# Four small moves in a fused retention and feed-forward kernel: attention of chunks 2 to 5 a tile later, one batch's transposes behind a matmul tile, one weight load triggered sooner, a last store of 128 columns

## The chip, the cores and the metric

The kernel runs on one core of a Trainium2 chip. The metric is the time of one execution on the device in microseconds (us). Six runs of the kernel before gave a median of 211.3 us, from 210.18 to 211.53. One further look at one execution, taken by the hardware profiler, gives the trace that this text reads.

## What is computed

Retention (a linear attention with a decaying state) over 4 batches, 8 heads, 768 positions and 64 dimensions a head; its output, with the heads side by side, is the 3072 x 512 input of a feed-forward layer with a tanh-approximated GELU:

```python
state = gamma * state + einsum('bhd,bhe->bhde', k[t], v[t])      # per head, for every t
y[t]  = scale * einsum('bhd,bhde->bhe', q[t], state)
x = y.transpose(0, 2, 1, 3).reshape(3072, 512)
h = x @ w_in                                                    # 512 -> 2048
out = gelu_tanh(h) @ w_out                                      # 2048 -> 512
```

## The kernel before, in words

**Tiling.** The 768 positions are cut into 6 chunks (c = 0 to 5) of 128; every chunk holds 4 batches (b), so 512 tokens. Per chunk the kernel does the attention in chunked form and then the two feed-forward products, M1 (x @ w_in, then GELU) and M2 (g @ w_out). The attention of chunk c + 1 is woven into the matmuls of chunk c, so that TensorE always has feed-forward tiles to work on while VectorE (DVE), ScalarE (ACT) and GpSimd (POOL) do the small steps of attention.

**Attention of one batch of one chunk.** `mm_T` transposes q and k on TensorE (chunks 0 and 1; from chunk 2 on `load_blk` loads q and k in blocks, POOL scales them in `prep_blk`, and `tr` transposes on DVE, L261). `mm_A` (L268) multiplies k and q into the scores, `ev_A` (L282) masks them on DVE, `mm_yc` (L289) adds what the state gives, `mm_yi` (L304) what the scores give, `ev_Y` (L317) copies the result into `xT`, which M1 reads; `mm_S` (L322) and `ev_S` (L340) make the next state, `decay` (L354) scales it on POOL. `att_AY` (L380) puts the scores of some batches and the outputs of others together, `att_Y` (L368) the outputs and states of all four.

**M1 and M2.** `moe1` (L452) and `moe1_two` (L457) make one M1 tile: matmuls into a PSUM bank and one GELU on ACT. `moe1_two` covers two column blocks for two batches: 8 matmuls of 256 columns. `units2` (L622) cuts the M2 work of one batch into 4 units of 4 matmuls of 512 columns; after the last of the four, `ev_O` (L495) copies the result to SBUF and stores it. `moe2_last` (L509) does the last batch of chunk 5 in two halves of 256 columns, each copied by DVE and stored by SP.

**What sets the order.** The program runs under a manual schedule: each engine does its instructions in the order in which the text emits them. `run(units, after)` (L521) emits a list of units, and behind unit i whatever the dictionary `after` has under i. In chunks 2 to 4 the units 0 to 15 are M1 tiles and 16 to 31 are M2 units. Loads of q, k and v sit on SP's queue (`load1`, `load_blk`, `load`), some on ACT's; the weights and most stores sit on POOL's, so that triggering a weight load is an instruction among POOL's other work. `hold` (L122, used at L609) makes SP's loads of chunk 1 wait until the third part of w_out has landed.

**The places that the change touches.**

- L545 to L551, on POOL: the first part of w_in is triggered, then k of batches 2 and 3 of chunk 0 is scaled (`prep1`, L195), then the other weight parts are triggered. Parts 0 and 1 of w_in are the two halves of the contraction rows of M1's first four column blocks: `m1a` (L594) uses part 0, and behind the attention of batch 3 part 1.
- L638 to L652: M2 of chunk 0 with attention of chunk 1. Behind its last unit come `att_AY` (which makes the y of batch 1, copied by ACT), `att_T(1, 3)` and `ev_S(1, 1)`.
- L671 to L687: M1 of chunk 1, first for batches 0 and 1, then for batches 2 and 3, 8 tiles each.
- L688 to L699 and L703 to L720: M2 of chunk 1, and chunks 2 to 4.
- L509 to L519: the last batch of the last chunk.

Of the kernel before, what the change touches and what calls it, by code (L numbers as in the profile page):

```python
# [16 lines left out]
def kernel(  # L17
# [14 lines left out]
    n_tok, d_model = out.shape  # L32
# [25 lines left out]
    att = ctx.enter_context(tc.tile_pool(name="att", bufs=4))  # L58
# [30 lines left out]
    def ld_tile(nm, c, b):  # L89
        if nm == "q":  # L90
            t = ld_all(("q32", c)).rearrange("p (b hp) a d -> p b (hp a d)", b=B)
            return t[:, b].rearrange("p (h d) -> p h d", h=H)
        if (nm, c, b) not in raw:
            raw[nm, c, b] = ld.tile([128, H, Dh], F32, tag=f"{nm}32", bufs=6, name=f"{nm}32")
        return raw[nm, c, b]
# [87 lines left out]
    def prep1(eng, nm, c, b):  # L183
        t = pre.tile(
            [128, H, Dh], F16, tag=f"{nm}16", bufs=6 if nm == "q" else 2 * B, name=f"{nm}16"
        )
        src = ld_tile(nm, c, b)
        if nm == "v":
            if eng is nc.scalar:
                eng.copy(out=t, in_=src)  # L190
            else:
                eng.tensor_copy(out=t, in_=src)  # L192
        else:
            col = OQ if nm == "q" else OK
            eng.tensor_tensor(  # L195
                out=t,
                in0=src,
                in1=cst[:, col:col + H].unsqueeze(2).broadcast_to([128, H, Dh]),
                op=ALU.mult,
            )  # L200
        h16[nm, c, b] = t
# [30 lines left out]
    def bank(tag, dt=F32, shape=(128, NHP, 128), name="ps"):  # L232
        return psum.tile(list(shape), dt, tag=tag, bufs=BANKS[tag], name=name)
# [168 lines left out]
    w_in_part = [(i, k, k + 2) for i in range(2) for k in (0, 2)]  # L402
# [14 lines left out]
    def load_w_in(n):  # L417
        i, k0, k1 = w_in_part[n]
        nc.gpsimd.dma_start(
            out=w_in_sb[n],  # L420
            in_=moe_w_in.rearrange("(kc p) (i n) -> p kc i n", p=128, i=NI)[:, k0:k1, i],
        )
# [29 lines left out]
    def moe1(c, fc):  # L452
        h_ps = bank("h", shape=(128, B * C), name="h_ps")
        moe1_mm(c, fc, h_ps, 0, B * C)
        gelu(g_tile(c, fc)[:, fc % 2], h_ps)
# [22 lines left out]
    def moe2_mm(ps, c, b, fcs, n0, n1):  # L478
        for fc in fcs:
            nc.tensor.matmul(  # L480
                out=ps[:, n0:n1],
                lhsT=g_sb[c, fc // 2][:, fc % 2, b * C:(b + 1) * C],
                rhs=w_out_sb[fc // (NF // NO)][:, fc % (NF // NO), n0:n1],
                start=(fc == 0),
                stop=(fc == NF - 1),
            )
# [21 lines left out]

    def moe2_last(c, b):  # L509

        hw = d_model // 2
        rows = out[b * S + c * C:b * S + (c + 1) * C, :]
        o_sb = op.tile([128, d_model], F32, tag="o", name="o_sb")
        for i in range(2):
            ps = bank("h", shape=(128, d_model), name="o_ps")
            m0, m2 = i * hw, (i + 1) * hw
            moe2_mm(ps, c, b, range(NF), m0, m2)
            nc.vector.tensor_copy(out=o_sb[:, m0:m2], in_=ps[:, m0:m2])  # L518
            nc.sync.dma_start(out=rows[:, m0:m2], in_=o_sb[:, m0:m2])  # L519

    def run(units, after):  # L521
        for i, u in enumerate(units):
            u()
            for f, *args in after.get(i, ()):
                f(*args)

    VE, AC, PO, SY = nc.vector, nc.scalar, nc.gpsimd, nc.sync
# [16 lines left out]
    nc.gpsimd.tensor_copy(out=misc[0:1, 4:5], in_=ld_tile("k", 0, 2)[0:1, 0, 0:1])  # L544
    load_w_in(0)  # L545
    prep1(PO, "k", 0, 2)
    prep1(PO, "k", 0, 3)
    for i in range(1, len(w_in_part)):
        load_w_in(i)
    for i in range(NO):  # L550
        load_w_out(i)  # L551
# [70 lines left out]
    def units2(c, b, n=4, tag="o"):  # L622
        u = [(lambda i=i: moe2(c, b, range(i, i + n), tag)) for i in range(0, NF, n)]
        last = u[-1]
        u[-1] = lambda: (last(), ev_O(c, b))
        return u
# [6 lines left out]
    for nm, b in (  # L633
# [12 lines left out]
            14: [(prep1, AC, "v", 1, 2), (att_T, 1, 2), (preps, 1, 3), (ev_S, 1, 0)],  # L646
            15: [
                (att_AY, 1, (1,), "h", 1, (2,), AC),
                (att_T, 1, 3),
                (ev_S, 1, 1),  # L650
            ],
        },  # L652
# [12 lines left out]
    def prep(c, nms):  # L665

        for nm in nms:
# [7 lines left out]
            for fp in range(NF // 2)  # L675
        ],
        {
            0: [(prep1, AC, "v", 1, 3)],
            1: [(att_AY, 1, (2,), "o", 1, (3,), VE)],
            3: [(ev_S, 1, 2)],  # L680
            4: [(att_AY, 1, (3,), "o", 1, (), VE)],
            6: [(ev_S, 1, 3)],
            7: [(prep, 2, "Q")],
            8: [(tr, 2, "q")],
# [4 lines left out]
        [x for b in range(B) for x in units2(1, b)],  # L689
        {  # L690
            1: [(tr, 2, "k", 0, 1)],
            3: [(att_AY, 2, (), "att", 2, (0, 1), None), (tr, 2, "k", 2, 3)],
            7: [(att_AY, 2, (), "att", 2, (2, 3), None)],
            12: [(att_Y, 2), (ev_S, 2, 0)],
            13: [(ev_S, 2, 1)],
            14: [(ev_S, 2, 2)],
            15: [(ev_S, 2, 3)],
        },
    )  # L699

# [1 line left out]
    for c in range(2, NCk - 1):  # L702
        n = c + 1  # L703
        after = {
            2: [(prep, n, "QKvk"), (tr, n, "q")],
            9: [(load, n + 1)] if n + 1 < NCk else [],
            16: [(tr, n, "k", 0, 1)],
            19: [(att_AY, n, (), "att", n, (0, 1), None), (tr, n, "k", 2, 3)],
            23: [(att_AY, n, (), "att", n, (2, 3), None)],
            27: [(att_Y, n)],  # L710
            28: [(ev_S, n, 0)],
            29: [(ev_S, n, 1)],
            30: [(ev_S, n, 2)],
            31: [(ev_S, n, 3)],
        }
        run(
            [(lambda fc=fc: moe1(c, fc)) for fc in range(NF)]
            + [x for b in range(B) for x in units2(c, b)],
            after,
        )  # L720
# [3 lines left out]
    for b in range(B - 1):  # L724
        for x in units2(c, b):
            x()
    moe2_last(c, B - 1)


# [28 lines left out]
```

## Time and profile before

| what | value |
|---|---|
| median of 6 runs (lowest to highest) | 211.3 us (210.18 to 211.53) |
| the profiled execution | 211.53 us, of which its span is 209.5 us |
| TensorE (PE) busy | 202.8 us, 97% of the span |
| DVE / ACT / POOL busy | 91.3 / 83.6 / 101.2 us |
| granted TensorE clock | 1.0 |
| matmuls of M1 (L435) and M2 (L480) | 84.7 and 86.8 us busy |
| DMA | 33.85 MB, mean 162 GB/s; 52.4% of the 16 engines' span on SP's queue |

A row of the timeline has the start in us from the span's start, the duration in us, the engine, the line, the operation with output and inputs, the shape and the count; in brackets stands how long the engine was idle before it, and what ended that. "PE" are matmuls, "PEld" weight loads, "SPq" the triggers of SP's DMA queue. Matmuls are pipelined: a row's duration reaches past the start of the next.

### The profile page before, as it was taken

How to read it: one execution, taken by the hardware profiler on the slowest of the kernel's cores; microseconds unless marked ns; L12 is line 12 of the kernel's file. 1: busy time of each engine (PE TensorE's matmuls, PEld its weight loads, DVE VectorE, ACT ScalarE, POOL GpSimd, SP SyncE). 2: the span in 40 equal slices, each digit the busy share in tenths (PEclk: the TensorE clock that was granted, in tenths of full speed). 3: DMA queues.
4: the chain of work that ended last, by engine and by line, in shares of the span. 5: the costliest groups of instructions: out<-in, count | busy, mean ns of one | idle time of the engine just before them, and what ended most of it. 6: DMA issues, size and time to landing. Idle time of an engine off the chain costs nothing.

```text
span 209.5 us, 4015 instructions
## 1 busy us (share of the span) xinstructions
PE 202.8 (97%) x1582; PEld 109.0 (52%) x1582; DVE 91.3 (44%) x163; ACT 83.6 (40%) x142; POOL 101.2 (48%) x123
## 2 busy tenths in 40 slices
PE   7996999999999999999999999999999999999994
PEld 2455544466888446444446444446444446444453
DVE  6698100188752774531776442476641472100001
ACT  2283662144656113466113466113466113466120
POOL 3597600325373966862958956681558821100100
PEclk9999999999999999999999999999999999999999
DMA  6999999997968999788989889989889121100112
GB/s 157 287 243 168 206 206 201 279 238 129 173 98 184 255 215 212 161 134 154 249 161 212 170 128 214 235 156 212 169 178 237 32 105 50 50 0 3 50 50 100
DMA packets 132691, 33.85 MB, mean 162 GB/s; under 512 B 126528, under 2 KB 130880, under 8 KB 132672
## 3 DMA queue, kind: packets, MB, share of 16 engines
q1 hardware_dynamic: 115248, 21.27, 52.4%
q0 software_dynamic: 5696, 8.91, 18.5%
q10 hardware_dynamic: 11728, 3.41, 7.1%
q8 instruction: 12, 0.20, 0.4%
q14 instruction: 7, 0.06, 0.1%
HBM read 31.48 MB, written 6.29 MB: 180 GB/s over the span
## 4 chain that ended last, share of the span: by engine, by line
PE 86%; DMA 10%; DVE 1%; POOL 1%; ACT 0%; issue 0%; SPq 0%
PE h_ps L435 39%; PE o_ps L480 39%; DMA k<-in_k_dram 5%; DMA w_in<-in_moe_w_in_dram 3%; PE a_ps L273 2%; PE y_ps L308 2%; DMA v<-in_v_dram 2%; PE y_ps L295 2%; PE s_ps L330 1%; POOL k L195 1%; PE qkT_ps L239 1%; DVE st L349 0%; DVE qkT L226 0%; ACT v L190 0%; DVE q L195 0%
## 5 line engine op out<-in xcount | busy, mean ns | idle before, releaser
L480 PE MATMUL o_ps<-w_out,g 128*128 128x512 f16 (+1 forms) x400 | 86.8, 371 | 0.0
L435 PE MATMUL h_ps<-xT,w_in 128*128 128x512 f16 (+1 forms) x464 | 84.7, 342 | 1.7 <-DMA w_in<-in_moe_w_in_dram 1.7
L450 ACT ACTIVATE g<-h_ps 128x512 f16<-128x512 f32 x96 | 56.8, 597 | 47.6 <-PE h_ps L435 47.5
L435 PEld LDWEIGHTS <-w_in 128*128 128x128 f16 x464 | 45.0, 98 | 39.5 <-DMA w_in<-in_moe_w_in_dram 1.8
L480 PEld LDWEIGHTS <-g 128*128 128x128 f16 x400 | 37.9, 98 | 41.0
L286 DVE TENSOR_TENSOR a_sb<-a_ps,mask 128x512 f16<-128x512 f32 x48 | 30.1, 683 | 15.0 <-PE a_ps L273 14.9
L502 ACT COPY o_sb<-o_ps 128x512 f32<-128x512 f32 x19 | 11.1, 586 | 58.1 <-PE o_ps L480 58.1
L195 POOL TENSOR_TENSOR k<-k,cst 128x512 f16<-128x512 f32 x23 | 23.8, 1056 | 12.3 <-DMA k<-in_k_dram 12.3
L507 POOL DMA_DIRECT2D out_dram<-o_sb x18 | 10.0, 559 | 34.6 <-ACT o_sb L502 23.9
L206 POOL TENSOR_TENSOR kT<-kT,cst 128x512 f16<-128x512 f32 x16 | 16.3, 1048 | 13.7 <-DMA kT<-in_k_dram 8.2
L356 POOL TENSOR_TENSOR stg<-st,cst 128x512 f32<-128x512 f16 x16 | 16.3, 1037 | 9.7 <-DVE st L349 8.0
L263 DVE STREAM_TRANSPOSE qkT<-kT 128x512 f16<-128x512 f16 x16 | 10.9, 697 | 16.2 <-POOL kT L206 16.2
L206 POOL TENSOR_TENSOR q<-q,cst 128x512 f16<-128x512 f32 x16 | 16.2, 1044 | 2.5 <-DMA kT<-in_k_dram 2.5
L263 DVE STREAM_TRANSPOSE qkT<-q 128x512 f16<-128x512 f16 x16 | 11.4, 711 | 14.0 <-POOL q L206 14.0
L349 DVE TENSOR_TENSOR st<-s_ps,stg 64x256 f16<-64x256 f32 x32 | 13.4, 420 | 0.8
L192 POOL CAST v<-v 128x512 f16<-128x512 f32 x16 | 9.6, 614 | 8.3 <-DMA v<-in_v_dram 8.2
L195 DVE TENSOR_TENSOR q<-q,cst 128x512 f16<-128x512 f32 x8 | 6.2, 769 | 17.0 <-DMA q<-in_q_dram 17.0
L226 DVE CAST xT<-y_ps 128x512 f16<-128x512 f32 x11 | 7.2, 687 | 14.0 <-PE y_ps L308 14.0
L518 DVE COPY o_sb<-o_ps 128x256 f32<-128x256 f32 x2 | 0.8, 425 | 26.6 <-PE o_ps L480 26.6
L171 PE MATMUL spin_ps<-zero 128*128 128x512 f16 x30 | 10.4, 493 | 1.3 <-DVE zero L139 1.3
L224 ACT CAST xT<-y_ps 128x512 f16<-128x512 f32 x13 | 7.2, 588 | 5.2 <-PE y_ps L308 5.1
L273 PE MATMUL a_ps<-qkT 64*128 64x128 f16 x192 | 8.1, 218 | 0.2
(39 smaller groups left out, 83.3 us busy)
## 6 DMA issues: line engine op xcount, KB each, us to landing
v<-in_v_dram SPq DMA_DIRECT2D x21, 256.0 KB, 4.5
k<-in_k_dram SPq DMA_DIRECT2D x20, 256.0 KB, 4.3
out_dram<-o_sb POOLq DMA_DIRECT2D x18, 256.0 KB, 3.1
q<-in_q_dram SPq DMA_DIRECT2D x64, 64.0 KB, 3.0
kT<-in_k_dram SPq DMA_DIRECT2D x64, 64.0 KB, 2.6
w_out<-in_moe_w_out_dram POOLq DMA_DIRECT2D x4, 512.0 KB, 15.8
q<-in_q_dram ACTq DMA_DIRECT2D x4, 256.0 KB, 7.8
k<-in_k_dram ACTq DMA_DIRECT2D x4, 256.0 KB, 7.6
```

Source lines behind the costliest of these rows:

```text
L171: nc.tensor.matmul(out=ps, lhsT=zero[:, 0:128], rhs=zero, start=True, stop=True)
L195: eng.tensor_tensor(out=t, in0=src, in1=cst[:, col:col + H].unsqueeze(2).broadcast_to([128, H, Dh]), op=ALU.mult,)
L206: nc.gpsimd.tensor_tensor(out=t, in0=ld_all((key, c))[:, b * NHP:(b + 1) * NHP].rearrange("p hp a d -> p (hp a) d"), in1=cst[:, col:col + ...
L263: nc.vector.transpose(out=qkT_tile(c, b)[:, "qk".index(nm)].rearrange("p hp t -> p (hp t)"), in_=blk16.pop((nm, c, b)).rearrange("p ha d - ...
L273: nc.tensor.matmul(out=ps[j][:, hp], lhsT=t[j * 64:(j + 1) * 64, 1, hp], rhs=t[j * 64:(j + 1) * 64, 0, hp], start=True, stop=True,)
L286: nc.vector.tensor_tensor(out=s, in0=ps[j], in1=mask[:, j], op=ALU.mult)
L349: nc.vector.tensor_tensor(out=st[sl, :, b, sl], in0=s_ps[sl], in1=stg[sl, :, b, sl], op=ALU.add)
L356: nc.gpsimd.tensor_tensor(out=stg[:, :, b], in0=st[:, :, b], in1=cst[:, OG:OG + NHP].unsqueeze(2).broadcast_to([128, NHP, 128]), op=ALU.mult,)
L435: nc.tensor.matmul(out=out, lhsT=w_in_of(fc, kc), rhs=xT[c][:, kc, t0:t1], start=(kc == 0 and first), stop=(kc == NHP - 1), skip_group_che ...
L450: nc.scalar.activation(out=out, in_=in_, func=AF.Gelu_apprx_tanh, scale=1.0)
L480: nc.tensor.matmul(out=ps[:, n0:n1], lhsT=g_sb[c, fc // 2][:, fc % 2, b * C:(b + 1) * C], rhs=w_out_sb[fc // (NF // NO)][:, fc % (NF // NO ...
L502: nc.scalar.copy(out=o_sb, in_=ps)
```

## The change

1. **The second part of w_in** is triggered on POOL ahead of the scaling of k of batch 3, not behind it.
2. **The transposes of batch 3 of chunk 1** (`att_T(1, 3)`) move from behind the last M2 unit of chunk 0 to behind the first M1 tile of chunk 1. The two `att_AY` of batches 2 and 3 in that M1 go one tile later each.
3. **Attention of chunks 2 to 5**: both score steps (`att_AY`) move one M2 unit later; in chunks 3 to 5 `att_Y` does too, and in chunk 2 it stays. The four `ev_S` each go one unit later, the last two together behind the last unit.
4. **The last batch of chunk 5** is cut into 384 and 128 columns, not 256 and 256.

```diff
-        hw = d_model // 2
+        cut = [0, d_model - 128, d_model]
...
-            m0, m2 = i * hw, (i + 1) * hw
+            m0, m2 = cut[i:i + 2]
...
     load_w_in(0)
     prep1(PO, "k", 0, 2)
+    load_w_in(1)
     prep1(PO, "k", 0, 3)
-    for i in range(1, len(w_in_part)):
+    for i in range(2, len(w_in_part)):
         load_w_in(i)
...
             15: [
                 (att_AY, 1, (1,), "h", 1, (2,), AC),
-                (att_T, 1, 3),
                 (ev_S, 1, 1),
             ],
...
-            0: [(prep1, AC, "v", 1, 3)],
-            1: [(att_AY, 1, (2,), "o", 1, (3,), VE)],
+            0: [(prep1, AC, "v", 1, 3), (att_T, 1, 3)],
+            2: [(att_AY, 1, (2,), "o", 1, (3,), VE)],
             3: [(ev_S, 1, 2)],
-            4: [(att_AY, 1, (3,), "o", 1, (), VE)],
+            5: [(att_AY, 1, (3,), "o", 1, (), VE)],
             6: [(ev_S, 1, 3)],
...
             1: [(tr, 2, "k", 0, 1)],
-            3: [(att_AY, 2, (), "att", 2, (0, 1), None), (tr, 2, "k", 2, 3)],
-            7: [(att_AY, 2, (), "att", 2, (2, 3), None)],
-            12: [(att_Y, 2), (ev_S, 2, 0)],
-            13: [(ev_S, 2, 1)],
-            14: [(ev_S, 2, 2)],
-            15: [(ev_S, 2, 3)],
+            4: [(att_AY, 2, (), "att", 2, (0, 1), None), (tr, 2, "k", 2, 3)],
+            8: [(att_AY, 2, (), "att", 2, (2, 3), None)],
+            12: [(att_Y, 2)],
+            13: [(ev_S, 2, 0)],
+            14: [(ev_S, 2, 1)],
+            15: [(ev_S, 2, 2), (ev_S, 2, 3)],
...
             16: [(tr, n, "k", 0, 1)],
-            19: [(att_AY, n, (), "att", n, (0, 1), None), (tr, n, "k", 2, 3)],
-            23: [(att_AY, n, (), "att", n, (2, 3), None)],
-            27: [(att_Y, n)],
-            28: [(ev_S, n, 0)],
-            29: [(ev_S, n, 1)],
-            30: [(ev_S, n, 2)],
-            31: [(ev_S, n, 3)],
+            20: [(att_AY, n, (), "att", n, (0, 1), None), (tr, n, "k", 2, 3)],
+            24: [(att_AY, n, (), "att", n, (2, 3), None)],
+            28: [(att_Y, n)],
+            29: [(ev_S, n, 0)],
+            30: [(ev_S, n, 1)],
+            31: [(ev_S, n, 2), (ev_S, n, 3)],
```

## The prediction

> **What bounds the kernel.** I read the page's busy times first, then TensorE's own waits, then the timeline around each wait and around the end.
>
> ```profile
> PE 202.8 (97%) x1582; PEld 109.0 (52%) x1582; DVE 91.3 (44%) x163; ACT 83.6 (40%) x142; POOL 101.2 (48%) x123
> ```
>
> TensorE (PE) is busy 97% of the 209.5 us span. So a change can win only where PE idles or behind its last matmul. TensorE's waits are few:
>
> ```profile
> PE h_ps L435 <- DMA w_in<-in_moe_w_in_dram: 1.7, 1, 1.7
> PE spin_ps L171 <- DVE zero L139: 1.3, 1, 1.3
> PE qkT_ps L239 <- DVE st L349: 0.3, 1, 0.3
> ```
>
> The middle one is the warm-up at the start. The first is the wait for the second part of w_in, the third the wait of the transposes that edit 2 moves. After 51 us PE never waits. The tail comes last: PE's last matmul ends at 206.41 us, 3.09 us ahead of the end. So there is about 1.7 + 0.35 us of idle time and a part of 3.1 us to win, against 211.53 us of the profiled execution (its span and 2.03 us around it). That execution is 0.23 us above the median of 211.3.
>
> **Edit 1, the second part of w_in.** The timeline of the start:
>
> ```profile
> 9.03 0.91 POOL L419 DMA_DIRECT2D w_in<-in_moe_w_in_dram  x1
> 9.96 1.05 POOL L195 TENSOR_TENSOR k<-k,cst 128x512 f16<-128x512 f32 x1
> 11.29 1.18 POOL L195 TENSOR_TENSOR k<-k,cst 128x512 f16<-128x512 f32 x1 [0.28 <-DMA k<-in_k_dram]
> 12.42 3.71 POOL L419 DMA_DIRECT2D w_in<-in_moe_w_in_dram  x5
> 13.17 0.40 PE L252 MATMUL qkT_ps<-iden,k 128*128 128x128 f16 x4
> 19.30 13.31 PE L435 MATMUL h_ps<-xT,w_in 128*128 128x256 f16 x72 [1.71 <-DMA w_in<-in_moe_w_in_dram]
> ```
>
> The first of the five triggers at 12.42 is part 1; it lands at 19.25, 6.83 us later. With the change it is triggered when k of batch 2 is scaled, at 11.02: 1.40 us sooner. If the landing moves as much, it is at 17.85 and PE waits 0.3 us, not 1.71: a gain of **1.40**. The bounds: 1.71 if the wait goes entirely, nothing if the landing stays.
>
> The trigger takes 0.77 us of POOL (0.91 for the one at 9.03). Scaling k of batch 3 then runs from 11.79 to about 12.95, not to 12.47; the 0.28 us wait for k goes. Its reader is the transpose that PE starts at 13.17, so 0.2 us of cover is left. If it ran over, PE's wait for w_in would take it up. The other weight triggers come at 12.95, not 13.18. What is late next: the landings of parts 2 and 3 (19.92 and 21.16) against PE's need of them at 21.9 and 23.7 less the lead; part 4 (23.71) is needed at 25.4 less the lead, so a lead up to 1.7 fits.
>
> What speaks against it is the DMA queue view between 9 and 13 us:
>
> ```profile
> q1 hardware_dynamic: 2486, 0.63, 69.5%
> q10 hardware_dynamic: 2089, 0.53, 58.3%
> ```
>
> Queue q0 (POOL's) is absent: part 0, triggered at 9.03, moves nothing before 13.2 us, when the loads of SP and ACT are through. By the packet times part 1 then follows part 0 on the engines without a gap, from 14.5 us. It would be done by 16 at full rate, but from 15.2 to 17 us the packets take up to 0.9 us in place of 0.1. Of its 16 completions 15 come by 17.41 us and one at 19.25. A sooner trigger changes nothing in that order; it helps if the slow packets come from descriptors that are written while they are read, since POOL writes triggers from 12.42 to 18.35 without a break.
>
> A rule of the Trainium skill speaks against edit 1 as well: "DMA: Bandwidth & Descriptors", section "Latency and other measured facts", says that two of the 16 DMA engines are usually slower in POOL-triggered transfers, as a best guess because the descriptor rings share their ports. One late completion of 16 agrees with it. By the rule the late engine stays late and the gain here would be near nothing.
>
> I take 1.40, the shift of the trigger, a little over even.
>
> **Edit 2, the transposes of batch 3.** The timeline between M2 of chunk 0 and M1 of chunk 1:
>
> ```profile
> 49.81 0.41 PE L308 MATMUL y_ps<-a_sb,v 128*64 128x128 f16 x8
> 50.26 0.59 ACT L224 CAST xT<-y_ps 128x512 f16<-128x512 f32 x1 [0.32 <-PE y_ps L308]
> 50.69 0.38 PE L239 MATMUL qkT_ps<-iden,q 128*128 128x128 f16 x4 [0.35 <-DVE st L349]
> 51.14 1.91 PE L435 MATMUL h_ps<-xT,w_in 128*128 128x256 f16 x16
> ```
>
> PE is through with y and the state product at 50.3, waits for DVE, transposes (0.45 us) and starts M1 at 51.14. M1's first tile reads batch 1 of xT, which ACT is copying until 50.85. Today the transposes cover that copy. With the change M1's tile stands first and waits for the copy: start at 50.91, and the transposes (0.45) come behind it. Up to the transposes and the tile PE is through 50.91 - 50.69 = **0.23 us later** than today. So this wait is not removed; it is exchanged for a longer one. Bounds: a gain of 0.35 if the tile did not wait, a loss of 0.5 if ACT's copy is late by 0.25 more. That can be: ahead of it on ACT stand the cast of v of batch 2 (47.94, released by its load) and a copy of M2's result, and if PE comes sooner but that load does not, the copy slips. The scores of batch 3 are three tiles behind the start, so DVE's eviction of the transposes (0.69) stays covered; so are the y copies of batch 3, now two M1 tiles (1.75 us) ahead of their readers and 0.7 us long.
>
> **Edit 3, attention a tile later.** No instruction is added, and PE does not wait there now: nothing by itself. It matters for what PE's lead runs into. SP's queue triggers without a gap from 44.5 us, whatever PE does, so the data of chunks 2 and 3 come no sooner:
>
> ```profile
> 69.59 0.71 DVE L263 STREAM_TRANSPOSE qkT<-kT 128x512 f16<-128x512 f16 x1 [0.30 <-POOL kT L206]
> 70.58 0.62 PE L273 MATMUL a_ps<-qkT 64*128 64x128 f16 x16
> 107.72 4.05 POOL L195 TENSOR_TENSOR k<-k,cst 128x512 f16<-128x512 f32 x4
> 112.08 0.67 PE L330 MATMUL s_ps<-v,k 128*64 128x64 f16 x32
> ```
>
> Chunk 2: k of batch 1 is transposed at 70.30, its scores start 0.28 us into the row, at 70.86: 0.56 us to spare. Chunk 3: k of batch 3 is scaled at 111.77, the second state product starts at 112.33: again 0.56. A tile later (4 matmuls of 0.2155 = 0.86 us) makes it 1.42 both times. A lead of 1.40 - 0.23 = 1.17 us fits; without edit 3 it would shrink to 0.56. State products of chunk 2 do not move: k is ready at 80.08, they need it at 81.73, 1.65 to spare. At the other end M1 of the next chunk starts 3 units (2.6 us) behind `att_Y`, not 4, and the xT copies take 1.3 us behind it: 1.3 us of cover is left. The last `ev_S` pair runs under M1. I take 0. The bounds: a loss of 0.35 (the one wait for a PSUM bank that the trace shows, at the transposes), and a gain of 0.35, since no PE wait of this size or more is there to remove.
>
> **Edit 4, the last store.**
>
> ```profile
> 205.14 2.11 SPq L519 DMA_DIRECT2D out_dram<-o_sb  x2
> 206.44 0.42 DVE L518 COPY o_sb<-o_ps 128x256 f32<-128x256 f32 x1 [1.32 <-PE o_ps L480]
> ```
>
> Of the tail, 0.42 is the copy of 256 columns; the 512-column copy of line 500 takes 0.69, so 128 columns take about 0.29: 0.13 sooner. The store of 128 KB is triggered at 206.89, its packets run from 207.75 to 208.25, 0.5 us; half as many bytes take 0.25. But the first store is now 192 KB (0.75 us) and starts at about 206.97, 0.86 us behind its trigger at 206.11, and ends at 207.72, so the second waits 0.1. Sum: 0.13 + 0.25 - 0.10 = **0.28 sooner**; bounds 0.1 (the copy alone) and 0.4. Matmuls of 384 and 128 columns cost PE the same as two of 256 (rows of 128 columns start every 0.055 us).
>
> **Sum.** -1.40 + 0.23 + 0 - 0.28 = -1.45: 210.08 us against the profile's 211.53, 209.85 against the median. I say **210.0**.
>
> **Rivals.**
>
> - *Part 1 lands when it did* (the order of the queue, the slow engine). Gain at the start 0 to 0.4, then +0.23 and -0.28: 211.1 to 211.5. For it speaks the queue view, against it that slow packets and triggers fall together.
> - *The copy decides, and the kernel gets slower.* The place is M1's first tile of chunk 1, the mechanism ACT's copy of batch 1 behind the cast of v of batch 2. With nothing won at the start, the load of v would have to land not at 47.9 but after 49.75 us: then cast, M2's copy and the xT copy (0.6 us each) end after 51.55, the tile starts 0.9 us or more behind today's place, and the total is +0.65 and more: 212.0 to 212.5. Against it: the load is triggered by ACT and has kept a 4.4 us landing.
> - *The wait at the start goes wholly*, 1.71: the lead is 1.48, chunk 2 takes 0.06 back: 209.6 to 209.8.
>
> **Chances.** My forecast with the neighbouring whole removal 0.52, landing unchanged 0.38, slower 0.10. A measurement of this kernel tells about 0.3% (0.63 us) from no change; the first is beyond it, the second within. Faster 0.52, same 0.38, slower 0.10. The first and second case hold the most, so the range reaches from a wholly removed wait with the larger tail gain (209.4) to the second case with a small loss (211.6). The forecast's own range is 209.4 to 210.5.
>
> **What would show it.** TensorE's wait for w_in: 0.3 us or none if right, 1.7 if the rival is. In its place at 49 to 51 us a wait of M1's first tile on ACT of about 0.6 us, and none of the transposes. No wait of PE at the scores of chunk 2 and the state products of chunk 3. The end 2.8 us behind the last matmul, not 3.09. Wrong would be: a new wait before the transposes at 13 us, or loads of chunk 1 that slip because ACT's come sooner.

## The result: 209.72 us, and the profile after

The changed kernel takes 209.72 us (median of 21 runs, 209.29 to 210.34). The kernel before, on the same chip in the same session, takes 210.9 us (47 runs, 210.17 to 212.5). The ratio is 0.9942, with a 95% interval from 0.9931 to 0.9954, so the change saves about 1.2 us. The profiled execution of the changed kernel took 209.72 us with a span of 207.7 us; that of the kernel before took 211.53 us with a span of 209.5 us.

The page's busy times first. They hardly move: the change removes idle time, not work.

```profile
PE 202.3 (97%) x1582; PEld 108.4 (52%) x1582; DVE 92.4 (44%) x163; ACT 83.8 (40%) x142; POOL 101.1 (49%) x123
```

TensorE's waits in the changed kernel (engine, line, what it waited for; us in total, times, the longest):

```profile
PE spin_ps L171 <- DVE zero L139: 1.3, 1, 1.3
PE h_ps L435 <- ACT xT L224: 0.6, 1, 0.6
PE qkT_ps L252 <- POOL k L195: 0.4, 1, 0.4
```

The wait of 1.7 us for w_in and the wait of 0.3 us for DVE's `st` are gone. In their place stand a wait for ACT's copy of `xT` and one for POOL's scaling of k. The timeline of the start:

```profile
9.66 1.58 POOL L195 TENSOR_TENSOR k<-k,cst 128x512 f16<-128x512 f32 x1
...
11.21 0.77 POOL L419 DMA_DIRECT2D w_in<-in_moe_w_in_dram  x1
...
11.99 1.05 POOL L195 TENSOR_TENSOR k<-k,cst 128x512 f16<-128x512 f32 x1
...
12.98 2.98 POOL L419 DMA_DIRECT2D w_in<-in_moe_w_in_dram  x4
...
13.11 0.40 PE L252 MATMUL qkT_ps<-iden,k 128*128 128x128 f16 x4 [0.41 <-POOL k L195]
...
17.46 6.89 PE L435 MATMUL h_ps<-xT,w_in 128*128 128x256 f16 x43
```

Part 1 of w_in is triggered at 11.21, not 12.42. M1 goes on at 17.46, not 19.30: 1.84 us sooner, more than the 1.71 us that TensorE had waited there. The 0.41 us wait at 13.11 is new. Part 1 lands at 16.67 us, 0.79 ahead of the matmul that needs it, so TensorE no longer waits for weights there, and the new wait stands in the chain of work that ended last (start, duration, engine and line):

```profile
11.25 0.72 POOL w_in L419
11.99 1.06 POOL k L195
13.11 0.40 PE qkT_ps L252 x4
```

Without it M1 could have gone on up to 0.41 us sooner (an estimate from these rows; no run tries it). The trace of edit 1 alone, further down, has no such wait and M1 goes on at 17.32, but so does the trace without edit 3, which has it.

The change from M2 of chunk 0 to M1 of chunk 1:

```profile
48.42 0.59 ACT L224 CAST xT<-y_ps 128x512 f16<-128x512 f32 x1 [0.31 <-PE y_ps L308]
...
49.06 1.03 PE L435 MATMUL h_ps<-xT,w_in 128*128 128x256 f16 x8 [0.55 <-ACT xT L224]
...
49.93 0.39 PE L239 MATMUL qkT_ps<-iden,q 128*128 128x128 f16 x4
...
50.37 1.91 PE L435 MATMUL h_ps<-xT,w_in 128*128 128x256 f16 x16
```

M1's first tile now waits 0.55 us for ACT. The transposes behind it wait for nothing.

The scores of chunk 2, where the prediction had read 0.56 us to spare:

```profile
68.08 0.71 DVE L263 STREAM_TRANSPOSE qkT<-kT 128x512 f16<-128x512 f16 x1 [0.29 <-POOL kT L206]
...
69.83 0.62 PE L273 MATMUL a_ps<-qkT 64*128 64x128 f16 x16
```

k of batch 1 is transposed at 68.79, and its scores start 0.28 us into the row, at 70.11: 1.32 us to spare, though TensorE starts M2 of chunk 1 1.61 us sooner than before.

The end:

```profile
204.51 0.99 SPq L519 DMA_DIRECT2D out_dram<-o_sb  x2
204.82 0.29 DVE L518 COPY o_sb<-o_ps 128x128 f32<-128x128 f32 x1 [0.34 <-PE o_ps L480]
```

The last copy takes 0.29 us where the one of 256 columns took 0.42. The last matmul ends at 204.79, and the execution ends 2.91 us behind it, where it was 3.09. The experiments' traces agree: 3.09 to 3.11 us in the five traces without edit 4, 2.90 to 2.92 in the nine with it.

So by these two traces the account is simple: 1.84 at the start, 0.18 at the end, and about 0.2 given back at chunk 1. That makes 1.8 us, more than the 1.2 us between the medians: the profiled execution of the kernel before, 211.53, is 0.63 us above that kernel's median. The experiments show that this account holds for the two profiled executions and is not what the other traces show.

### The profile page after: what moved, and what is told of

Read it like the earlier page. It is cut to its first block, busy times and chain, and to the rows that moved or that the text cites. A ratio compares the mean times of both kernels' runs of the same rounds, so it can differ in the third digit from the quotient of the medians.

```text
span 207.7 us, 4013 instructions
## 1 busy us (share of the span) xinstructions
PE 202.3 (97%) x1582; PEld 108.4 (52%) x1582; DVE 92.4 (44%) x163; ACT 83.8 (40%) x142; POOL 101.1 (49%) x123
## 4 chain that ended last, share of the span: by engine, by line
PE 92%; DMA 3%; POOL 2%; SPq 1%; ACT 0%; issue 0%; DVE 0%
PE o_ps L480 41%; PE h_ps L435 40%; PE a_ps L273 3%; DMA k<-in_k_dram 3%; PE y_ps L308 3%; PE y_ps L295 2%; POOL k L195 1%; PE s_ps L330 1%; PE qkT_ps L239 1%; POOL w_in L419 1%; SPq L98 1%; PE spin_ps L171 0%; PE qkT_ps L252 0%; ACT xT L224 0%; SPq L126 0%
## 5 line engine op out<-in xcount | busy, mean ns | idle before, releaser
L480 PE MATMUL o_ps<-w_out,g 128*128 128x512 f16 (+2 forms) x400 | 86.8, 371 | 0.0
L480 PEld LDWEIGHTS <-g 128*128 128x128 f16 x400 | 37.3, 98 | 41.7
L206 POOL TENSOR_TENSOR kT<-kT,cst 128x512 f16<-128x512 f32 x16 | 16.3, 1049 | 12.5 <-DMA kT<-in_k_dram 5.9
L263 DVE STREAM_TRANSPOSE qkT<-q 128x512 f16<-128x512 f16 x16 | 11.4, 711 | 12.3 <-POOL q L206 12.2
L195 DVE TENSOR_TENSOR q<-q,cst 128x512 f16<-128x512 f32 x8 | 7.0, 870 | 15.7 <-DMA q<-in_q_dram 15.7
L518 DVE COPY o_sb<-o_ps 128x384 f32<-128x384 f32 (+1 forms) x2 | 0.8, 424 | 26.4 <-PE o_ps L480 26.4
L171 PE MATMUL spin_ps<-zero 128*128 128x512 f16 x30 | 9.9, 470 | 1.3 <-DVE zero L139 1.3
```

The costliest lines, as they stand in the source:

```text
L195: eng.tensor_tensor(out=t, in0=src, in1=cst[:, col:col + H].unsqueeze(2).broadcast_to([128, H, Dh]), op=ALU.mult,)
L206: nc.gpsimd.tensor_tensor(out=t, in0=ld_all((key, c))[:, b * NHP:(b + 1) * NHP].rearrange("p hp a d -> p (hp a) d"), in1=cst[:, col:col + ...
L263: nc.vector.transpose(out=qkT_tile(c, b)[:, "qk".index(nm)].rearrange("p hp t -> p (hp t)"), in_=blk16.pop((nm, c, b)).rearrange("p ha d - ...
L480: nc.tensor.matmul(out=ps[:, n0:n1], lhsT=g_sb[c, fc // 2][:, fc % 2, b * C:(b + 1) * C], rhs=w_out_sb[fc // (NF // NO)][:, fc % (NF // NO ...
```

## The experiments

Theory 1 is the prediction's: the wait for w_in is the loss, the sooner trigger (edit 1) removes it, and moving the attention (edit 3) is worth nothing by itself. The rival: TensorE's place is set by the loads of chunks 2 and 3 on SP's queue; edit 3 carries the gain, and edit 1 alone runs into those loads. Each kernel was timed in five rounds beside the kernel before on its own chip. That kernel's median was 211.95, 212.0 and 211.32 us in the three groups, so only ratios are compared between groups. The three groups ran on three chips; the one trace of the kernel before was taken apart from them. Each variant has one trace, of one of its runs.

### One edit at a time (kernel before: 211.95 us)

**Edit 1 alone.**

```diff
     prep1(PO, "k", 0, 2)
+    load_w_in(1)
     prep1(PO, "k", 0, 3)
-    for i in range(1, len(w_in_part)):
+    for i in range(2, len(w_in_part)):
```

> Edit 1 alone. Theory A (the sooner trigger takes the wait for the second part of w_in away; the other edits matter little): 0.8 to 1.6 us faster than the kernel before, TensorE's wait for w_in 0 to 0.3 us, and a wait of up to 0.4 us ahead of the transposes at 13 us. Without edit 3 the lead runs into the scores of chunk 2 or the state products of chunk 3 with 0.56 us to spare there, so a wait of some tenths can show there. Rival B (the second part lands when its queue lets it, whatever the trigger): the same time within 0.3 us, and the wait of 1 to 1.7 us still there.

Measured: 210.72 us (12 runs, 210.19 to 212.63), ratio 0.9946 [0.9917, 0.9976]. The profiled execution is the fastest of the twelve. No wait for w_in is left, and none ahead of the transposes at 13 us. In its place comes one at the scores of chunk 3, behind DVE's transposes, which the kernel before did not show:

```profile
PE qkT_ps L239 <- DVE st L349: 0.5, 1, 0.5
PE a_ps L273 <- DVE qkT L263: 0.3, 1, 0.3
```

**Edit 2 alone.**

```diff
                 (att_AY, 1, (1,), "h", 1, (2,), AC),
-                (att_T, 1, 3),
                 (ev_S, 1, 1),
...
-            0: [(prep1, AC, "v", 1, 3)],
-            1: [(att_AY, 1, (2,), "o", 1, (3,), VE)],
+            0: [(prep1, AC, "v", 1, 3), (att_T, 1, 3)],
+            2: [(att_AY, 1, (2,), "o", 1, (3,), VE)],
             3: [(ev_S, 1, 2)],
-            4: [(att_AY, 1, (3,), "o", 1, (), VE)],
+            5: [(att_AY, 1, (3,), "o", 1, (), VE)],
```

> Edit 2 alone. Theory A: 0.2 us slower (0.1 to 0.3): the wait of the transposes (0.35 us) is gone, a wait of M1's first tile for ACT's copy (0.55 to 0.6 us) has come. Rival B (removing the wait of the transposes is where the gain comes from): 0.3 us or more faster.

Measured: 212.16 us (12 runs), ratio 1.002 [0.9989, 1.0051]: the expected 0.2 us, but it can't be told from nothing. The profiled execution, 212.64 us, has a long list of waits:

```profile
PE a_ps L273 <- DVE qkT L263: 1.7, 4, 0.6
...
PE h_ps L435 <- ACT xT L224: 0.6, 1, 0.6
PE s_ps L330 <- POOL k L195: 0.4, 1, 0.4
PE h_ps L435 <- DMA w_in<-in_moe_w_in_dram: 0.4, 1, 0.4
```

The wait for w_in is 0.4 us here, though this kernel triggers it as late as before: the same trigger gives a different wait in another execution. What TensorE gained by that it lost at the scores of chunks 2 and 3 and the state products of chunk 3. The timeline at chunk 2:

```profile
67.42 4.06 POOL L206 TENSOR_TENSOR kT<-kT,cst 128x512 f16<-128x512 f32 x4 [4.04 <-DMA kT<-in_k_dram]
...
69.51 0.71 DVE L263 STREAM_TRANSPOSE qkT<-kT 128x512 f16<-128x512 f16 x1 [0.29 <-POOL kT L206]
...
70.27 0.40 PE L273 MATMUL a_ps<-qkT 64*128 64x128 f16 x8 [0.61 <-DVE qkT L263]
```

POOL waited 4.04 us for the load of `kT`, DVE for POOL, TensorE for DVE. The load is the origin; the two engines only pass it on.

**Edit 3 alone**, here for chunks 3 to 5, and in the same way for chunk 2 as in the change:

```diff
-            19: [(att_AY, n, (), "att", n, (0, 1), None), (tr, n, "k", 2, 3)],
-            23: [(att_AY, n, (), "att", n, (2, 3), None)],
-            27: [(att_Y, n)],
+            20: [(att_AY, n, (), "att", n, (0, 1), None), (tr, n, "k", 2, 3)],
+            24: [(att_AY, n, (), "att", n, (2, 3), None)],
+            28: [(att_Y, n)],
```

> Edit 3 alone. Theory A: no difference (within 0.15 us), since TensorE does not wait at the attention of chunks 2 to 5 as long as it has no lead. Rival C (a tile's distance to the data is worth something by itself, or is lost at the end of a chunk): 0.3 us or more to either side, with a wait in chunks 2 to 5.

Measured: 210.51 us (11 runs), ratio 0.9934 [0.9906, 0.9962]. The expectation was missed, and this is the surprise of the study: the part that I had put at nothing gains 1.4 us alone, as much as the whole change. Its waits are two, both at their old places:

```profile
PE h_ps L435 <- DMA w_in<-in_moe_w_in_dram: 1.0, 1, 1.0
PE qkT_ps L239 <- DVE st L349: 0.3, 1, 0.3
```

**Edit 4 alone.**

```diff
-        hw = d_model // 2
+        cut = [0, d_model - 128, d_model]
...
-            m0, m2 = i * hw, (i + 1) * hw
+            m0, m2 = cut[i:i + 2]
```

> Edit 4 alone. Theory A: 0.2 us faster (0.1 to 0.3): 0.13 us from the shorter copy and little from the smaller store. Rival D (the store's fixed time decides and the larger first store stands in its way): no difference or slower.

Measured: 211.9 us (12 runs), ratio 0.9998 [0.9972, 1.0025]: a tenth or two can't be told from nothing here. The profiled execution again has what the kernel before did not show, though nothing ahead of the last tile was touched:

```profile
PE a_ps L273 <- DVE qkT L263: 1.5, 3, 0.6
...
PE h_ps L435 <- DMA w_in<-in_moe_w_in_dram: 0.7, 1, 0.7
```

So these waits belong to the kernel before, in other executions. Its one profiled execution was free of them, and had the longest wait for w_in of all (1.7 us). Whether that lies in the execution or in the chip is not shown: that kernel has only this one trace.

### The change without one edit (kernel before: 212.0 us)

**Without edit 2** (against the changed kernel):

```diff
                 (att_AY, 1, (1,), "h", 1, (2,), AC),
+                (att_T, 1, 3),
                 (ev_S, 1, 1),
...
-            0: [(prep1, AC, "v", 1, 3), (att_T, 1, 3)],
-            2: [(att_AY, 1, (2,), "o", 1, (3,), VE)],
+            0: [(prep1, AC, "v", 1, 3)],
+            1: [(att_AY, 1, (2,), "o", 1, (3,), VE)],
```

> Edits 1, 3 and 4, without edit 2. Theory A: 0.2 us faster than the full change, so 1.4 us faster than the kernel before (1.2 to 1.7); the wait of the transposes (0.35 to 0.4 us) is back, that of M1's first tile for ACT is gone. Rival B (edit 2 is part of the gain): 0.3 us slower than the full change.

Measured: 209.82 us (6 runs, 209.4 to 210.69), ratio 0.9907 [0.9878, 0.9936]. The wait for `st` is back (0.6 us) and that for ACT is gone. The full change did not run in this group; where it did, it took 209.72 and 209.82 us, so edit 2 adds no gain that can be seen.

**Without edit 3**: the lines of edit 3 above, back to units 19, 23 and 27.

> Edits 1, 2 and 4, without edit 3. Theory A: the lead of 0.9 to 1.6 us shrinks to what chunks 2 and 3 leave (0.56 us by the trace before, more where SP's loads came sooner as well), so 0 to 0.7 us slower than the full change, with waits at the scores of chunk 2 or the state products of chunk 3. Rival C (edit 3 does nothing): the same as the full change.

Measured: 211.28 us (12 runs, 209.96 to 211.76), ratio 0.9961 [0.9937, 0.9986], 1.46 us above the version without edit 2 on the same chip. Most of the gain goes with edit 3, and more than the 0 to 0.7 us that was expected. The runs spread over 1.8 us; the profiled one is among the fast (210.19) and loses about 0.3 us each at the scores of chunks 2 and 3. What the slow ones lose, no trace shows.

**Part 1 with a gap behind its trigger.** The prediction held that the slow packets of part 1 come from POOL writing further triggers meanwhile. This kernel is the kernel before, with one scaling whose result is unused (1.06 us) between the trigger of part 1 and that of part 2:

```diff
-    for i in range(1, len(w_in_part)):
+    load_w_in(1)
+    gap = const.tile([128, H, Dh], F16, name="gap")
+    nc.gpsimd.tensor_tensor(out=gap, in0=ld_tile("k", 0, 3), ...)
+    for i in range(2, len(w_in_part)):
```

> The kernel before, with the trigger of the second part of w_in where it was, and one more scaling on POOL (1.05 us, its result unused) between it and the next trigger. If the slow packets of the second part come from the triggers that follow it at once (the rings are written while they are read), its last completion comes at 16.5 to 17.5 us and the kernel is 0.7 to 1.4 us faster, as with the sooner trigger. If the distance from its own trigger to its turn is what counts, the landing stays at 18 to 19.3 us and the time the same, or up to 0.3 us slower since the later parts come 1 us later.

Measured: 212.87 us (12 runs), ratio 1.0041 [1.0016, 1.0067]. Part 1 lands at 17.48 us, at the edge of what the first theory asks for (16.5 to 17.5) and also among the landings of the late trigger elsewhere (17.34 to 19.25), so the landing alone decides nothing. The packets do, the pieces of 1 KB in which the DMA moves the weights. Part 0 is the first 256 of POOL's queue, so the next 256 in order of start are part 1, nearly all. Of these, 31 took over 150 ns here, 25 to 34 in the five other traces with the late trigger, and 0 to 2 in the eight with the sooner one. (Counted over all weights it is less clear: 53 to 83 against 5 to 27, but 56 in one trace with the sooner trigger.) The gap ends at 14.30 us and POOL writes on beside part 1's packets, which start at about 14.7; but so it does in the changed kernel, from 12.98 to 18.9 us, where only one of these packets is slow. So triggers that follow are not what slows part 1. The gap delays the weights behind it: TensorE waits for w_out, and SP's loads start later.

```profile
PE a_ps L273 <- DVE qkT L263: 1.2, 2, 0.6
PE o_ps L480 <- DMA w_out<-in_moe_w_out_dram: 0.7, 2, 0.5
```

**The new wait for ACT taken away.** The full change, with the y of batch 1 made one M2 unit sooner, so that ACT's copy is done when M1 starts:

```diff
-            14: [(prep1, AC, "v", 1, 2), (att_T, 1, 2), (preps, 1, 3), (ev_S, 1, 0)],
+            14: [(prep1, AC, "v", 1, 2), (att_T, 1, 2), (preps, 1, 3),
+                 (att_AY, 1, (1,), "h", 1, (), AC), (ev_S, 1, 0)],
             15: [
-                (att_AY, 1, (1,), "h", 1, (2,), AC),
+                (att_AY, 1, (), "h", 1, (2,), AC),
```

> The full change, and in addition the y of batch 1 of chunk 1 is made ahead of the last M2 unit of chunk 0, not behind it, so that ACT's copy runs under that unit. Theory A (edit 2 put M1's first tile in front of a copy that it waits for): the wait of 0.55 us is gone, 0.5 us faster than the full change (0.3 to 0.6), 1.7 us faster than before, if the lead then still fits chunks 2 and 3. Rival: another thing is late in its place (the scores of batch 2, DVE) and the time stays within 0.2 us of the full change.

Measured: 209.73 us (6 runs), ratio 0.9898 [0.987, 0.9926]. The wait for ACT is gone from the trace: ACT's copy starts at 47.39 and M1 follows without a wait. Whether the time is gained is left to the next group, where the full change runs beside it.

```profile
47.39 0.59 ACT L224 CAST xT<-y_ps 128x512 f16<-128x512 f32 x1 [0.72 <-PE y_ps L308]
...
48.71 1.05 PE L435 MATMUL h_ps<-xT,w_in 128*128 128x256 f16 x8
```

### The full change beside its variants (kernel before: 211.32 us)

**The full change once more.**

> The full change, beside its variants on one chip. Theory (the median of the kernel before differs from chip to chip, 210.9 to 212.0, because its waits differ from execution to execution, and that of the full change does not): 209.7 to 209.9 us here as before, ratio 0.990 on a chip where the kernel before takes 212, 0.994 where it takes 210.9; TensorE waits 0.5 to 0.6 us for ACT's copy at 49 us and 0.4 us for k at 13 us, nowhere else. Rival (the ratio is that of the two kernels, whatever the chip): 0.994 also where the kernel before takes 212, so 210.7.

Measured: 209.82 us (6 runs, 209.66 to 210.41), ratio 0.993 [0.991, 0.9951]. TensorE waits where it was expected, and once more for k (two such waits, 0.9 us in total). The changed kernel took 209.72 and 209.82 us the two times, the kernel before beside it 210.9 and 211.32, as the theory has it. It isn't shown: the interval also holds 0.994, the rival's ratio, and the full change was not run where the kernel before takes 212.

**The covered copy once more**, the kernel of the diff above.

> The full change with the y of batch 1 of chunk 1 made ahead of the last M2 unit of chunk 0, now beside the full change on one chip. Theory (the 0.55 us that M1's first tile waits for ACT is idle time that nothing takes up later): 0.3 to 0.5 us below full_again. Rival (the lead of 0.5 us ends at the scores of chunk 2, where the data come when they come): within 0.1 us of full_again, with a wait of TensorE for DVE at 68 to 71 us or for POOL at 113 us.

Measured: 210.05 us (6 runs, 209.39 to 210.73), ratio 0.9927 [0.9903, 0.9951]. It can't be told from the full change, and the theory's 0.3 to 0.5 us below it is not seen. The profiled execution is the slowest of the six, and shows the rival at work: SP's loads of chunk 2 start at 44.66 us here, against 43.74 in the changed kernel's trace above, and the data of chunk 3 come late for the state products, even a tile later. The wait:

```profile
112.62 0.32 PE L330 MATMUL s_ps<-v,k 128*64 128x64 f16 x8 [0.41 <-POOL k L195]
```

**The change without edit 1**: POOL's order as it was, edits 2 to 4 in place.

```diff
     prep1(PO, "k", 0, 2)
-    load_w_in(1)
     prep1(PO, "k", 0, 3)
-    for i in range(2, len(w_in_part)):
+    for i in range(1, len(w_in_part)):
```

> Edits 2, 3 and 4 without edit 1: the price of the sooner trigger when the attention stands a tile later. Theory (the wait for w_in is 0.4 to 1.7 us with the late trigger, 0 with the early one, and with edit 3 in place nothing behind it takes that back): 0.4 to 1.7 us above full_again, about 0.9, with that wait in the list of TensorE's waits. Rival (edit 3 alone was worth 1.4 us, so edit 1 adds nothing to it): within 0.2 us of full_again.

Measured: 210.05 us (6 runs, 209.91 to 210.33), ratio 0.9939 [0.9919, 0.9959]. That is 0.23 us above the full change, not 0.4 to 1.7: the expectation was missed. With edit 3 in place, the edit that my prediction rested on is worth a few tenths at most, and six runs of each can't tell it from nothing. The trace shows where they are, a short wait for w_in and a touch of the scores of chunk 3:

```profile
17.60 2.58 PE L435 MATMUL h_ps<-xT,w_in 128*128 128x256 f16 x22 [0.40 <-DMA w_in<-in_moe_w_in_dram]
```

```profile
101.89 0.23 PEld L273 LDWEIGHTS <-qkT 64*128 64x128 f16 x8 [0.25 <-DVE qkT L263]
```

**Scores two units later** on top of the covered copy:

```diff
-            20: [(att_AY, n, (), "att", n, (0, 1), None), (tr, n, "k", 2, 3)],
-            24: [(att_AY, n, (), "att", n, (2, 3), None)],
+            21: [(att_AY, n, (), "att", n, (0, 1), None), (tr, n, "k", 2, 3)],
+            25: [(att_AY, n, (), "att", n, (2, 3), None)],
```

> copy_covered_again with both score steps of chunks 2 to 5 one more M2 unit later (att_Y and the state evictions stay). Theory (the lead still touches the data of chunks 2 and 3 by a few tenths in some executions): 0 to 0.3 us below copy_covered_again, no wait of TensorE at the scores. Rival (the steps behind the scores get too short: ev_A and the outputs of att_Y, three units later instead of four): slower by 0.3 us or more, with waits of TensorE for DVE's a_sb at the outputs of each chunk.

Measured: 209.92 us (6 runs, 209.23 to 210.22), ratio 0.9926 [0.9902, 0.995]. The profiled execution has no wait of TensorE behind the transposes of chunk 0 and is the shortest trace of the study (209.23 us), but the median is that of its neighbours. No version here is shown to beat the full change.

### All traces side by side

Four numbers of each trace tell what happened. "M1 resumes": the start of the first matmul on part 1 of w_in. "Loads": SP's trigger of the first block of chunk 2. "Distance": the start of M2 of chunk 1 less that trigger, that is, how long the loads have before TensorE gets to them. "Lost": what the stretch from there to M1 of chunk 3 takes beyond 49.11 us (17.65 to M1 of chunk 2 and 31.46 to that of chunk 3), its length in the undisturbed traces. All in us.

| kernel | M1 resumes | loads | distance | lost |
|---|---|---|---|---|
| *without edit 3* | | | | |
| before | 19.30 | 44.54 | 22.49 | 0.0 |
| edit 1 alone | 17.32 | 43.51 | 21.74 | 0.44 |
| without edit 3 (1, 2, 4) | 17.32 | 43.66 | 21.61 | 0.59 |
| edit 2 alone | 17.39 | 44.53 | 20.80 | 2.82 |
| gap behind the trigger | 18.05 | 46.09 | 20.71 | 1.83 |
| edit 4 alone | 17.97 | 45.27 | 20.62 | 2.13 |
| *with edit 3* | | | | |
| full again | 17.38 | 43.49 | 21.83 | 0.0 |
| edit 3 alone | 18.46 | 44.47 | 21.73 | 0.0 |
| without edit 2 | 17.58 | 43.84 | 21.70 | 0.0 |
| after | 17.46 | 43.74 | 21.68 | 0.0 |
| scores two later | 17.48 | 43.73 | 21.20 | 0.0 |
| covered copy | 17.62 | 44.02 | 21.13 | 0.08 |
| covered copy again | 17.65 | 44.66 | 21.02 | 0.68 |
| without edit 1 (2, 3, 4) | 17.60 | 44.59 | 20.95 | 0.25 |

Each row is one execution, so this is a pattern and not a law: the distance doesn't fix the loss to better than a microsecond (20.71 and 20.80 us cost 1.83 and 2.82). Three things can be read. First, without edit 3 a distance of 21.6 to 21.7 us already costs about half a microsecond and 20.6 to 20.8 costs 1.8 to 2.8; with edit 3, 21.7 costs nothing and 21.0 costs 0.3 to 0.7. The distance at which losses begin has moved by about 0.7 us, near the one M2 unit of 0.86 by which edit 3 moves the scores. Second, the loss is all at chunks 2 and 3: from M1 of chunk 3 to the start of M2 of chunk 5 all fourteen traces take 76.24 us, with edit 3 or without. Third, the loads move with edit 1. SP's queue is held until the third part of w_out has landed, and that part stands behind w_in on POOL's queue. SP's triggers of the kernel before:

```profile
34.93 0.37 SPq L98 DMA_DIRECT2D q<-in_q_dram  x1
...
44.54 2.05 SPq L110 DMA_DIRECT2D q<-in_q_dram  x2
```

and of the changed kernel:

```profile
34.27 0.37 SPq L98 DMA_DIRECT2D q<-in_q_dram  x1
...
43.74 2.23 SPq L110 DMA_DIRECT2D q<-in_q_dram  x2
```

The third part of w_out lands at 34.01 us, not 34.68, SP starts 0.66 us sooner, and the loads of chunk 2 come 0.80 us sooner. Over all traces it lands at 33.75 to 34.29 us with the sooner trigger, once at 35.07, and at 34.68 to 35.63 with the late one (36.65 with the gap).

## Why the prediction was right, and where it was not

The time, 210.0 us forecast and 209.72 measured, and the sign were right: 1.3 us below 211.3 was forecast, 1.2 below 210.9 was measured. The reasons were right in part.

- **Edit 1, the step right, its cause wrong, its size that of one execution.** The landing moved with the trigger: in the two profiled executions by 2.58 us for 1.21, on the mean of all traces by 1.31 for 1.27. Part 1 lands at 16.53 to 17.04 us in the eight traces with the sooner trigger, and at 17.34 to 19.25 in the six with the late one. In the two profiled executions that is worth 1.84 us. But the 1.71 us wait was the longest of all; in the other traces with the late trigger it was 0.4 to 1.0 us, or none in the trace with the gap. On the mean of the traces M1 resumes at 18.13 us with the late trigger and at 17.48 with the sooner: 0.65 us. The cause that I gave, triggers written while packets are read, fell: POOL writes triggers beside part 1's packets with the sooner trigger too, and they are not slow. What goes with the slow packets in the traces is the distance from the trigger to the first packet: part 1 moves from about 14.6 to 14.8 us, a little over 2 us behind the late trigger and over 3 behind the sooner one. Why packets are slow when that distance is short stays open.
- The rule of the Trainium skill that I weighed against edit 1, "DMA: Bandwidth & Descriptors", section "Latency and other measured facts" (two of the 16 DMA engines are usually slower in POOL-triggered transfers), did not decide. The last of part 1's 16 completions came 1.84 us behind the 15th in the kernel before, but 0.01 to 1.10 behind in the other late ones, and 0.02 to 0.38 with the sooner trigger.
- **Edit 1, the wait at 13 us.** I had 0.2 us of cover there and named a new wait as a sign of being wrong. The wait came, 0.41 us, since POOL's scaling of k took 1.58 us and not 1.05. The remark that TensorE's wait for w_in would take it up failed: no wait for w_in was left, and the chain that ended last runs through the wait for k. The change won in spite of it.
- **Edit 2, right.** M1's first tile waits 0.55 us for ACT. From the start of M2 of chunk 0 to that of chunk 1 it is 34.82 us, not 34.59: 0.23 us later, the term as predicted (50.91 less 50.69 is 0.22). In other traces without edit 2 that stretch is 34.77 to 34.81 us in three, two of which wait 0.5 to 0.6 for `st`; it is 34.59 with edit 3 alone and 35.60 with the gap, where w_out is late. So the part costs between 0.2 us and nothing, and the times can't tell it from nothing.
- **Edit 3, wrong.** The step that failed is "PE does not wait there now: nothing by itself", with bounds of 0.35 on either side. Alone it gained 1.4 us (0.9934), and taking it out of the change lost it again. The runs showed waits at chunks 2 and 3 in its place, up to 2.8 us in total. The one trace showed none because it has the longest distance between the loads and their use, 22.49 us. In the trace of edit 4 alone, the kernel before up to its last tile, it is 20.62: the wait for w_in is 1.0 us shorter there, so TensorE starts M2 of chunk 1 at 65.89 and not 67.03, and the loads come 0.73 us later. The margins that I read off it, 0.56 us twice, were margins of that execution. They were noted and then used only for the lead of edit 1, not for the spread between executions.
- **Edit 3, a second step.** "The data of chunks 2 and 3 come no sooner" failed too: they came 0.80 us sooner, by way of the hold on w_out. By the table this is why the lead of edit 1 fits: without it the distance would be 20.88 us, not 21.68 (no run separates the two).
- **Edit 4, mis-sized.** 0.18 us in the trace, not 0.28. The copy gave its 0.13. The store gave 0.05 where I had 0.15: from the trigger of the last store to its completion it took 1.65 us with 64 KB and 1.70 with 128 KB.

That the sum came out is in part luck: the term for edit 1 holds for one execution and that for edit 3 was wrong, and the two made up for each other, because the losses at the start and at chunks 2 and 3 exclude each other in part. The one execution that waited 1.7 us for w_in did not wait for the loads later. Alone, edit 1 gained 0.54% and edit 3 0.66%, and their intervals overlap; together with the two small ones it is 0.6 to 0.7% the two times that the full change ran. The trace of before put all of it on the first place. By the medians either edit alone gives nearly the whole: taking edit 3 out cost 1.46 us beside the version without edit 2, taking edit 1 out 0.23 beside the full change.

## What to carry to other kernels

A wait that a trace does not show can be one that another wait of the same execution hides: ask of each margin behind a long wait what it is when that wait is short. Where one engine's work meets a stream of loads that another queue paces, take the distance between the two over several executions, not over one, and give it more slack than the spread; that was worth as much here as removing the longest wait in the list. And a step that is moved on one queue moves what is held by that queue's later transfers.

## What the runs showed of the hardware

**A scaling on POOL and one on DVE hold each other up.** In the changed kernel the POOL scaling of k took 1.58 us where it took 1.05 before, and so triggered part 1 at 11.21 and not at the 11.02 that I had worked out. With edit 1 alone it took 1.05, and DVE's scaling of q took 1.37 instead of 0.68, as in the kernel before. With edit 1 alone:

```profile
9.76 1.05 POOL L195 TENSOR_TENSOR k<-k,cst 128x512 f16<-128x512 f32 x1
10.01 1.37 DVE L195 TENSOR_TENSOR q<-q,cst 128x512 f16<-128x512 f32 x1
```

In the changed kernel DVE's row starts 0.01 us behind POOL's, and POOL is the one that is lengthened:

```profile
9.66 1.58 POOL L195 TENSOR_TENSOR k<-k,cst 128x512 f16<-128x512 f32 x1
9.67 0.68 DVE L195 TENSOR_TENSOR q<-q,cst 128x512 f16<-128x512 f32 x1
```

In both, the second to get through ends 0.6 to 0.9 us behind the first. The Trainium skill has a rule for it: "SBUF — State Buffer", section "SBUF: two separate sides", says that the two engines share a pair of ports as an exclusive lock. Of a DVE instruction with two SBUF inputs and a POOL instruction that reads SBUF, the one that starts first has the pair for its whole duration. The rows of edit 1 alone agree with that. In the changed kernel one is held up as well, but by its row POOL started first, by 0.01 us, and lost. It can reach TensorE: in the second trace of the covered copy DVE's scaling of q at 47.53 took 1.52 us instead of the 1.02 of the first, and the scores of batch 3 came 0.5 us later (52.72 against 52.19).

**A late weight trigger has no fixed landing.** Triggered at 12.3 to 12.5 us, part 1 landed between 17.34 and 19.25 us; triggered at 10.75 to 11.40, between 16.53 and 17.04. The medians of the kernel before spread from group to group (210.9 to 212.0 us), those of the full change less (209.72 and 209.82, two groups alone). That the landing is the reason is argued from the traces and not tested by itself.
